# First loads of a recurrent attention and mixture-of-experts kernel, reordered: the first chunk's decay in two transfers, the third chunk's decay ahead of a value tile

## The chip, the cores and the metric

The kernel runs on one core of one Trainium2 chip. The metric is the device time of one execution in microseconds. Of the kernel before, three runs took 281.44, 281.70 and 282.26 us; their median is 281.7 us.

## The reference

There are two stages. The first is a linear attention with a decaying state, for 4 batches, 8 heads, 768 positions and a head size of 48:

```python
for t in range(S):
    cur = einsum('bhd,bhe->bhde', u * k[t], v[t])
    y[t] = einsum('bhd,bhde->bhe', r[t], state + cur)
    state = w[t][..., None] * state + einsum('bhd,bhe->bhde', k[t], v[t])
```

The second takes the 3072 rows of y, 384 wide. A row whose product with `w_skip` is not positive stays as it is. The others go to the one expert of eight with the largest logit of `x @ w_gate`, and get `gate * (relu(x @ w1[e]) @ w2[e])` added, where the gate is that expert's softmax share; the hidden width is 1024.

## The kernel before, in words

**Tiling.** The positions are cut into chunks of 128, six for each batch, 24 in all. `seq` lists them in the order in which they are worked; "chunk 0" below is the first of that list. A chunk has the eight heads as four pairs on 128 partitions. Its arrays w, r, k (`wrk`) lie behind one another in a row: first w (columns 0 to `R_OFF`, 521 words, four groups of `CW` = 130), then r (512 words, up to `K_OFF`), then k (512 words, up to `V_OFF`). Three SBUF buffers `wrk_sb` take chunks in turn; v comes twice, turned (`vt`, two transfers for each chunk) and plain (`v`).

**One chunk's work.** `prep_scan` (L300) runs a backward scan on VectorE (DVE) that makes q, the running product of w. `prep_keys` (L320) makes kq = k*q on GpSimd (POOL) and a reciprocal on DVE that is written into the w tile. `prep_reads` (L327) makes a forward scan rh on DVE and rp = r*rh on POOL. `bonus_keys` (L315) makes rk = r*k on POOL: for chunks 0 and 1 behind rp, for later ones ahead of kq. On TensorE (PE), `scores` (L352) multiplies kq with rp into `psA`, `bonus_sums` (L375) sums rk into `psY`, and `rows_of_keys` (L342) transposes kq, which ScalarE (ACT) copies out as kt. DVE masks the two score tiles (`mask`, L361) and multiplies `psY` with the turned v (`bonus`, L380). `update` (L383) adds to the state from kt and v, `outputs` (L403) adds masked scores times v and state times rp into `psY`, `evict` (L416) copies that out on ACT, and `rows_out` (L421) turns it into rows and router logits by a product with `wgp_sb`, which holds identity columns and router columns.

**Order.** Everything is written by hand: each engine works its instructions in the order of the program. The loop `for s in range(-2, n + 1)` (L681) works on several chunks in one step: it issues loads for chunk s+4 (`load_chunk`) and s+3 (`load_turned`, `load_v`), then update(s), prep_scan(s+2), outputs(s), prep_keys(s+2), prep_reads(s+2), evict(s), scores(s+1), bonus_sums(s+1), rows_of_keys(s+1), the masks and the bonus of s+1, and rows_out(s). So DVE's queue has the scans of chunk s+2 ahead of the masks of chunk s+1. Ahead of the loop, `setup` (L238) issues the loads of chunks 0 to 2 and the memsets, and `fill` (L672) gives PE products of zeros to do. All loads of this stage go through SyncE's (SP) queue, but for u, which is issued from ScalarE.

**Loads at the start, in SP's order.** Chunk 0's w, its r and k in one; chunk 1's w, a table of constants, its r and k; the turned v of chunk 0 in two, its plain v, and chunk 2 in one transfer of 1545 words a row (L178); the router columns in four transfers of 36-byte pieces (L687); turned v and v of chunk 1; chunk 3.

**After the attention** come the router's last products and eight experts, one after the other, with weights split into a high and a low part.

Of the kernel before, what the change touches and what calls it, by code (L numbers as in the profile page):

```python
# [8 lines left out]
F32 = mybir.dt.float32  # L9
# [6 lines left out]
ALU = mybir.AluOpType  # L16
# [5 lines left out]
P = 128  # L22
# [35 lines left out]
def rwkv_moe_kernel(ctx, tc, wrk, wrk0, vN, uP, wgs, wgp, w12, cst, out):  # L58
# [83 lines left out]
    with tc.tile_pool(name="att", bufs=2) as att, \  # L142
# [7 lines left out]
        def half(g, n_=HP):  # L150
            return slice(HP * g, HP * g + n_)

        def shifted(eng, dst, src):

            eng.dma_start(dst[HP:], src[HP:])
            eng.dma_start(dst[KO:HP], src[:D])
            eng.dma_start(dst[:KO], src[D:HP])

        def load_vt(eng, vt, i, o):
            b, c = seq[i]  # L160
            z = wrk[b, c, 0, :, V_OFF + o * 2 * P:V_OFF + (o + 1) * 2 * P]
# [3 lines left out]
        def load_turned(i):  # L165
            for o in range(2):
                load_vt(nc.sync, vt_sb[i % (NBUF + 1)], i, o)

        def load_chunk(i):
            b, c = seq[i]  # L170
            rows = wrk.rearrange("b c g d n -> (b c g d) n")
            at = 2 * D * chunk[i]
            t = wrk_sb[i % NBUF]
            to, at = (t, at - KO) if 0 < chunk[i] < n - 1 else (t[KO:LO], at)
            for cs in (slice(0, R_OFF), slice(R_OFF, V_OFF)) if i < 2 else (slice(0, V_OFF),):
                if i == 1 and cs.start > 0:
                    nc.sync.dma_start(c_sb[:, :C_IOTA], cst[:, :C_IOTA])
                nc.sync.dma_start(to[:, cs], rows[at:at + to.shape[0], cs])  # L178

        def load_v(i):  # L180
            b, c = seq[i]
            v_sb[i] = att.tile([P, H, D], F32, tag="v", name=f"v{i}", bufs=4)
            nc.sync.dma_start(v_sb[i], vN[b, c])
# [11 lines left out]
        identb = keep.tile([P, P], BF16, name="identb")  # L195
        tok = c_sb[:, C_TOK:C_TOK + 2 * B * NC].rearrange("p (c q) -> p c q", q=2)
        rows1_ = c_sb[:, C_HS + 3:C_HS + 4]
        wgp_sb = keep.tile([P, NP, XW], F32, name="wgp_sb")
        wgp_half = wgp_sb.rearrange("p (s g) x -> p g s x", g=2)
        wgs_sb = keep.tile([P, KC, E + 1], F32, name="wgs_sb")  # L200
        ends = keep.tile([P, n, NP], F32, name="ends")
        lows = keep.tile([P, n, NP], F32, name="lows")
# [33 lines left out]
        count_w = scratch(1)  # L236

        def setup():  # L238
            for t in vt_sb[:3]:
                nc.gpsimd.memset(t, 0.0)  # L240
            load_chunk(0)
            load_chunk(1)
            load_turned(0)
            load_v(0)
            load_chunk(2)
            shifted(nc.scalar, u_sb, uP)
            nc.gpsimd.memset(wgp_sb, 0.0)
            nc.gpsimd.memset(vt_sb[3], 0.0)
            nc.gpsimd.memset(onesb, 1.0)
            nc.gpsimd.memset(ohs, 0.0)  # L250
            nc.gpsimd.memset(key, 0.5)
            nc.vector.memset(warm, 0.0)
            nc.vector.memset(pss, 0.0)
            ints = ones_w.bitcast(U32)
            for a in range(NP):
                at = (a + 1) * CW - 1
                nc.vector.memset(ints[:, at // 4:at // 4 + 1], 1 << 8 * (at % 4))
            nc.vector.memset(rowsk, 1.0)
            nc.vector.memset(rowsk[:KO], 0.0)
            nc.vector.memset(rowsk[96:], 0.0)  # L260
            nc.vector.memset(rowsk[96:LO], 1.0)
            nc.vector.tensor_scalar(reads_w.bitcast(U32), ints, rowsk, None, op0=ALU.mult)
            nc.scalar.activation(junk0, warm[:, 0:1], AF.Exp)
            for z in psa:
                nc.scalar.copy(z.rearrange("p a j -> p (a j)"), warm)
            for o in range(2):
                eye = ident[half(o, D), HP * o:HP * o + D]
                for g in range(2):
                    c0 = (o ^ g) * D
                    nc.scalar.copy(wgp_half[half(o, D), g, :, c0:c0 + D],  # L270
                                   eye.rearrange("p (s x) -> p s x", s=1).to_broadcast([D, 2, D]))
            nc.scalar.copy(ubk_sb, u_sb.rearrange("p (a o) -> p a o", o=1).to_broadcast([P, NP, D]))
            for g in range(2):
                nc.tensor.matmul(psy2[:, g].rearrange("p s j -> p (s j)"), warm[:, :P], warm,
                                 start=True, stop=True, skip_group_check=True)
            nc.tensor.matmul(psu.rearrange("p a j -> p (a j)"), warm[:, :P], warm[:, :NP * HP],
                             start=True, stop=True, skip_group_check=True)
# [22 lines left out]
        def prep_scan(i):  # L300
            wk = work[i] = {}
            t = wrk_sb[i % NBUF]
            n_ = NP * CW
            a3 = lambda z: z.rearrange("p (a j) -> p a j", a=NP)
            wk["w"] = t
            wk["r"], wk["k"] = a3(t[:, R_OFF:K_OFF]), a3(t[:, K_OFF:V_OFF])
            q = wk["q"] = att.tile([P, NP, CW], F32, tag="q", name=f"q{i}", bufs=2)
            nc.vector.tensor_tensor_scan(  # L308
                q.rearrange("p a j -> p (a j)")[:, ::-1], t[:, 1:1 + n_][:, ::-1],
                ones_at[:, 1:1 + n_][:, ::-1], 0.0, op0=ALU.mult, op1=ALU.max)  # L310
            rk = wk["rk"] = att.tile([P, NP, P], F32, tag="rk", name=f"rk{i}")
            if i > 1:
                bonus_keys(i)
# [107 lines left out]
        def rows_out(i):  # L421
            psx = work[i]["psx"] = ps1.tile([P, NP, P], F32, tag="psT", name=f"psX{i}", bufs=2)
            xT = work[i]["xT"]
            for a in range(NP):
                nc.tensor.matmul(psx[:, a, :XW], xT[:, a], wgp_sb[:, a], start=True, stop=True)  # L425

        def store(i):
            psx = work.pop(i)["psx"]
# [243 lines left out]
        def fill(k, w=512):  # L672
            psw = ps1.tile([P, 512], F32, tag="psT", name="psw", bufs=2)
            for _ in range(k):
                nc.tensor.matmul(psw[:, :w], warm[:, :P], warm[:, :w], start=True, stop=True)

        with tc.manual_schedule():
# [3 lines left out]
            for s in range(-2, n + 1):  # L681
                on = lambda i: 0 <= i < n
                if s == -2:
                    for o in range(2):
                        for g in range(2):
                            at = 2 * (g ^ o)
                            nc.sync.dma_start(wgp_half[half(o), g, :, 2 * D:],  # L687
                                              wgp[half(g), at:at + 2, 2 * D:])
                if 3 <= s + 4 < n:
                    load_chunk(s + 4)  # L690
                if on(s + 3) and s + 3 >= 1:
                    load_turned(s + 3)
                    load_v(s + 3)
# [413 lines left out]
```

## Time and profile before

| | us |
|---|---|
| median of three runs | 281.7 |
| the profiled execution | 282.66 |
| its span, first to last instruction | 280.8 |
| PE busy in it | 266.0 |
| DVE, ACT, POOL busy | 212.6, 158.1, 146.5 |

The span counts from the first to the last instruction; the execution's own time has 1.86 us more around it. A busy PE counts products of zeros as well, and a product at half the clock counts for as long as it takes. The rows further down have the start of an instruction, counted from the span's start, and its length, both in us; a bracket at the end says how long the engine stood idle ahead of it and which engine's work ended last before it started. That name is inferred.

### The profile page before, as it was taken

The numbers are of one execution on the slowest core, as the hardware profiler recorded it, in microseconds if no ns is written. First come the engines' busy times: TensorE is split into PE (matmuls) and PEld (weight loads), VectorE is DVE, ScalarE is ACT, GpSimd is POOL, SyncE is SP. The second block draws the span as 40 slices with busy tenths as digits, with TensorE's granted clock in tenths as the row PEclk, the third lists the DMA queues.
The fourth block names the chain that finished last, engine by engine and source line by source line (L and its number), as shares of the span: only waits on it lengthen the run. The fifth ranks groups of instructions, "written<-read, shape, count | busy, mean of one in ns | idle before, by whom it ended". The sixth has DMA issues, their size and how long they took to land.

```text
span 280.8 us, 8941 instructions
## 1 busy us (share of the span) xinstructions
PE 266.0 (95%) x3599; PEld 245.0 (87%) x3599; DVE 212.6 (76%) x399; ACT 158.1 (56%) x460; POOL 146.5 (52%) x139
## 2 busy tenths in 40 slices
PE   7879999998999999899999999999999999999992
PEld 2668888897878887787989999999999999999992
DVE  7688999999999999982646787876849578595320
ACT  4436646785688857786427482745818367391300
POOL 6977677798899996894555744011030110301111
PEclk9989999999999999999999999999999999999997
DMA  7999999999977999972058998767563656700001
GB/s 248 231 316 322 314 317 358 358 326 320 277 237 221 303 331 371 254 252 86 30 132 301 350 306 288 243 233 251 180 237 98 247 229 223 250 28 28 9 5 41
DMA packets 26162, 64.23 MB, mean 229 GB/s; under 512 B 4334, under 2 KB 15524, under 8 KB 26112
## 3 DMA queue, kind: packets, MB, share of 16 engines
q1 hardware_dynamic: 23888, 58.27, 63.1%
q0 software_dynamic: 2048, 5.30, 6.1%
q8 instruction: 30, 0.49, 0.7%
q14 instruction: 20, 0.16, 0.2%
q10 hardware_dynamic: 176, 0.00, 0.0%
HBM read 56.52 MB, written 7.67 MB: 229 GB/s over the span
## 4 chain that ended last, share of the span: by engine, by line
PE 59%; issue 5%; ACT 3%; DVE 2%; DMA 1%; POOL 1%; POOLq 0%; DVEq 0%; ACTq 0%
PE psO L915 7%; PE psO L917 6%; PE psO L916 6%; PE psH L890 6%; PE psH L889 6%; PE psH L891 6%; PE psH L135 4%; PE psY L409 3%; PE psX L425 3%; PE psA L358 2%; PE psT L348 2%; PE psY L377 2%; PE psY L413 2%; PE psX L819 2%; DMA xg<-out,idr 1%
## 5 line engine op out<-in xcount | busy, mean ns | idle before, releaser
L826 POOL DMA_INDIRECT out<-fin,ids x16 | 16.6, 1039 | 95.9 <-DVE fin L924 88.9
L896 ACT ACTIVATE hh<-psH 128x240 fp32r<-128x240 f32 (+1 forms) x60 | 22.4, 374 | 53.6 <-PE psH L891 47.6
L890 PE MATMUL psH<-xTl,w1h 128*128 128x240 f32 x168 | 46.3, 275 | 0.0
L889 PE MATMUL psH<-xTh,w1h 128*128 128x240 f32 x168 | 46.1, 275 | 0.0
L891 PE MATMUL psH<-xTh,w1l 128*128 128x240 f32 x168 | 46.1, 274 | 0.0
L915 PE MATMUL psO<-w2h,hh 128*128 128x384 f32 (+1 forms) x120 | 40.9, 341 | 0.0
L917 PE MATMUL psO<-w2h,hl 128*128 128x384 f32 (+1 forms) x120 | 40.3, 335 | 0.0
L916 PE MATMUL psO<-w2l,hh 128*128 128x384 f32 (+1 forms) x120 | 40.2, 335 | 0.0
L364 DVE TENSOR_TENSOR asb<-psA,c_sb 128x512 f32<-128x512 f32 x48 | 30.6, 680 | 5.4 <-PE psA L358 5.2
L901 DVE SCALAR_TENSOR_TENSOR hl<-psH,hh 128x240 fp32r<-128x240 f32 (+1 forms) x60 | 24.3, 405 | 12.7 <-ACT hh L896 8.7
L325 POOL TENSOR_TENSOR kq<-wrk,q 128x512 f32<-128x512 f32 x24 | 28.4, 1185 | 10.0 <-DVE q L308 6.3
L330 DVE TENSOR_TENSOR_SCAN rh<-wrk,rowsk,pss 128x520 f32<-128x520 f32 x24 | 31.1, 1296 | 2.1
L308 DVE TENSOR_TENSOR_SCAN q<-wrk,pss 128x520 f32<-128x520 f32 x24 | 29.5, 1230 | 4.1 <-ACT xT L418 2.2
L334 POOL TENSOR_TENSOR rp<-wrk,rh 128x512 f32<-128x512 f32 x24 | 28.5, 1187 | 6.5 <-DVE rh L330 5.6
L891 PEld LDWEIGHTS psH<-xTh,w1l 128*128 128x128 f32 x168 | 31.8, 189 | 0.0
L889 PEld LDWEIGHTS psH<-xTh,w1h 128*128 128x128 f32 x168 | 31.7, 189 | 0.0
L890 PEld LDWEIGHTS psH<-xTl,w1h 128*128 128x128 f32 x168 | 31.7, 189 | 0.0
L317 POOL TENSOR_TENSOR rk<-wrk 128x512 f32<-128x512 f32 x24 | 30.7, 1278 | 2.0 <-DMA wrk<-wrk 1.6
L409 PE MATMUL psY<-asb,v 128*48 128x128 f32 x384 | 27.1, 277 | 4.4 <-DVE psY L381 4.2
L91 DVE TENSOR_TENSOR w2l<-r,w2h 128x512 fp32r<-128x512 f32 x42 | 27.7, 685 | 1.7 <-ACT w2h L90 1.5
L418 ACT COPY xT<-psY 128x512 f32<-128x512 f32 x24 | 14.1, 588 | 26.0 <-PE psY L413 22.7
L358 PE MATMUL psA<-rp,kq 64*64 64x128 f32 (+1 forms) x768 | 26.6, 256 | 1.4 <-POOL rp L334 1.0
(153 smaller groups left out, 592.7 us busy)
## 6 DMA issues: line engine op xcount, KB each, us to landing
r<-w SPq DMA_DIRECT2D x48, 512.0 KB
wrk<-wrk SPq DMA_DIRECT2D x20, 772.5 KB
vt<-wrk SPq DMA_DIRECT2D x48, 96.0 KB
v<-vN SPq DMA_DIRECT2D x24, 192.0 KB
out<-x SPq DMA_DIRECT2D x24, 192.0 KB
wrk<-wrk SPq DMA_DIRECT2D x2, 579.4 KB
wrk<-wrk SPq DMA_DIRECT2D x2, 512.0 KB
wrk<-wrk SPq DMA_DIRECT2D x2, 260.5 KB
```

The costliest lines, as they stand in the source:

```text
L308: nc.vector.tensor_tensor_scan(q.rearrange("p a j -> p (a j)")[:, ::-1], t[:, 1:1 + n_][:, ::-1], ones_at[:, 1:1 + n_][:, ::-1], 0.0, op0= ...
L317: nc.gpsimd.tensor_tensor(work[i]["rk"].rearrange("p a j -> p (a j)"), t[:, R_OFF:K_OFF], t[:, K_OFF:V_OFF], op=ALU.mult)
L330: nc.vector.tensor_tensor_scan(rh.rearrange("p a j -> p (a j)"), wk["w"][:, 0:NP * CW], reads_at[:, :NP * CW], rowsk, op0=ALU.mult, op1=AL ...
L358: nc.tensor.matmul(psa[g][j:j + HP, a, j:], wk["kq"][rows, a, j:j + HP], wk["rp"][rows, a, j:], start=True, stop=True)
L364: nc.vector.tensor_tensor(s, psa[g], tri.rearrange("p (o j) -> p o j", o=1).to_broadcast([P, NP, P]), op=ALU.mult)
L409: nc.tensor.matmul(y_at(a, g), v[:, 2 * a + g], wk["asb"][g][:, a], start=False, stop=True, skip_group_check=True)
L889: nc.tensor.matmul(ps, w1h[:, o:o + P], xTh[:, kc], start=(kc == 0), stop=False)
L890: nc.tensor.matmul(ps, w1h[:, o:o + P], xTl[:, kc], start=False, stop=False)
L891: nc.tensor.matmul(ps, w1l[:, o:o + P], xTh[:, kc], start=False, stop=(kc == KC - 1))
L915: nc.tensor.matmul(po, h[j, fc][0], w2h[:, o], start=(fc == 0), stop=False)
L916: nc.tensor.matmul(po, h[j, fc][0], w2l[:, o], start=False, stop=False)
L917: nc.tensor.matmul(po, h[j, fc][1], w2h[:, o], start=False, stop=(fc == FC - 1))
```

## The change

The changed kernel cuts chunk 0's `wrk` into four transfers: the first two groups of w, the other two, k, r. The scan that makes q of chunk 0 becomes two scans, one for each half of w. Chunk 2's `wrk` becomes two transfers; its w is issued ahead of the plain v of chunk 0, its r and k behind that v. u is loaded with two transfers in place of three, into a tile that POOL has cleared. The router columns and identity come in three transfers in place of four: for partitions 0 to 63 rows of 840 bytes that hold both, for the others router columns alone, so ScalarE makes two copies of the identity in place of four, and `wgp_sb` changes its layout. The second `fill` of step -1 has three short products in place of two.

```diff
-            for cs in (slice(0, R_OFF), slice(R_OFF, V_OFF)) if i < 2 else (slice(0, V_OFF),):
-                if i == 1 and cs.start > 0:
-                    nc.sync.dma_start(c_sb[:, :C_IOTA], cst[:, :C_IOTA])
-                nc.sync.dma_start(to[:, cs], rows[at:at + to.shape[0], cs])
+        w_half = 1 + NP * CW // 2
+        cuts = {0: ((0, w_half), (w_half, R_OFF), (K_OFF, V_OFF), (R_OFF, K_OFF)),
+                1: ((0, R_OFF), (R_OFF, V_OFF)), 2: ((0, R_OFF), (R_OFF, V_OFF))}
...
+            for c0, c1 in cuts.get(i, ((0, V_OFF),)):
+                yield nc.sync.dma_start(to[:, c0:c1], rows[at:at + to.shape[0], c0:c1])
...
         def setup():
+            nc.gpsimd.memset(u_sb, 0.0)
             for t in vt_sb[:3]:
                 nc.gpsimd.memset(t, 0.0)
-            load_chunk(0)
-            load_chunk(1)
+            drain(load_chunk(0))
+            second, third = load_chunk(1), load_chunk(2)
+            next(second)
+            nc.sync.dma_start(c_sb[:, :C_IOTA], cst[:, :C_IOTA])
+            next(second)
             load_turned(0)
+            next(third)
             load_v(0)
-            load_chunk(2)
-            shifted(nc.scalar, u_sb, uP)
-            nc.gpsimd.memset(wgp_sb, 0.0)
+            next(third)
+            nc.scalar.dma_start(u_sb[HP:LO], uP[HP:LO])
+            nc.scalar.dma_start(u_sb[KO:HP], uP[:D])
+            nc.gpsimd.memset(wgp_sb[HP:], 0.0)
...
-            nc.vector.tensor_tensor_scan(
-                q.rearrange("p a j -> p (a j)")[:, ::-1], t[:, 1:1 + n_][:, ::-1],
-                ones_at[:, 1:1 + n_][:, ::-1], 0.0, op0=ALU.mult, op1=ALU.max)
+            for c0, c1 in ((0, n_),) if i else ((0, n_ // 2), (n_ // 2, n_)):
+                nc.vector.tensor_tensor_scan(
+                    q.rearrange("p a j -> p (a j)")[:, c0:c1][:, ::-1], t[:, 1 + c0:1 + c1][:, ::-1],
+                    ones_at[:, 1 + c0:1 + c1][:, ::-1], 0.0, op0=ALU.mult, op1=ALU.max)
...
-                    for o in range(2):
-                        for g in range(2):
-                            at = 2 * (g ^ o)
-                            nc.sync.dma_start(wgp_half[half(o), g, :, 2 * D:],
-                                              wgp[half(g), at:at + 2, 2 * D:])
+                    z = wgp[half(0), :2]
+                    z = bass.AP(z.tensor, z.offset,
+                                [z.ap[0], [(HP * NP + 2) * XW, 2], [1, 2 * XW]])
+                    nc.sync.dma_start(wgp_sb[half(0)].rearrange("p g s x -> p g (s x)"), z)
+                    for g in range(2):
+                        at = 2 * (g ^ 1)
+                        nc.sync.dma_start(wgp_sb[half(1), g, :, 2 * D:],
+                                          wgp[half(g), at:at + 2, 2 * D:])
...
                     if s == -1:
                         fill(2)
-                        fill(2, 8)
+                        fill(3, 8)
```

## Rows read from the trace of the kernel before

**Rows 1.** By stretch: length; busy PE, PEld, DVE, ACT, POOL; PEclk, DMA share, GB/s.
```profile
12.50:15.00 2.50, 2.50 (x59) 2.31 (x56) 1.80 (x3) 2.37 (x7) 1.83 (x2) 1.00 0.47 90
15.00:18.60 3.60, 1.75 (x33) 1.53 (x34) 3.29 (x5) 0.82 (x5) 2.35 (x3) 0.98 1.05 343
18.60:22.00 3.40, 3.40 (x68) 3.04 (x66) 2.23 (x4) 1.67 (x6) 2.95 (x3) 0.52 1.05 322
22.00:35.00 13.00, 13.00 (x272) 11.47 (x262) 12.12 (x17) 8.38 (x31) 8.75 (x9) 1.00 1.06 321
130.00:275.00 145.00, 144.18 (x1114) 142.34 (x1113) 96.88 (x209) 74.32 (x173) 38.65 (x35) 1.00 0.53 180
```

**Rows 2.** TensorE in order of time, 7 to 30 us.
```profile
7.71 1.09 PE L358 MATMUL psA<-rp,kq 64*64 64x128 f32 x32 [1.03 <-POOL rp L334]
...
10.85 0.61 PE L390 MATMUL psu<-v,kt 128*64 128x48 f32 x15
...
12.32 1.09 PE L358 MATMUL psA<-rp,kq 64*64 64x128 f32 x32
...
15.24 0.67 PE L390 MATMUL psu<-v,kt 128*64 128x48 f32 x16
17.75 1.35 PE L409 MATMUL psY<-asb,v 128*48 128x128 f32 x16 [1.85 <-DVE psY L381]
...
24.13 0.30 PE L409 MATMUL psY<-asb,v 128*48 128x128 f32 x1
...
29.01 0.30 PE L409 MATMUL psY<-asb,v 128*48 128x128 f32 x1
```

**Rows 3.** VectorE in order of time: the scans of q, masks, bonus.
```profile
3.55 1.24 DVE L308 TENSOR_TENSOR_SCAN q<-wrk,pss 128x520 f32<-128x520 f32 x1 [0.51 <-DMA wrk<-wrk]
...
13.06 1.24 DVE L308 TENSOR_TENSOR_SCAN q<-wrk,pss 128x520 f32<-128x520 f32 x1 [2.24 <-ACT xT L418]
...
15.83 1.26 DVE L364 TENSOR_TENSOR asb<-psA,c_sb 128x512 f32<-128x512 f32 x2
17.01 0.69 DVE L381 TENSOR_TENSOR psY<-psY,vt 128x512 f32<-128x512 f32 x1
18.01 1.24 DVE L308 TENSOR_TENSOR_SCAN q<-wrk,pss 128x520 f32<-128x520 f32 x1 [0.31 <-DMA wrk<-wrk]
...
23.70 1.23 DVE L308 TENSOR_TENSOR_SCAN q<-wrk,pss 128x520 f32<-128x520 f32 x1
```

**Rows 4.** GpSimd in order of time: chunk 0's kq, chunk 2's rk.
```profile
5.35 1.17 POOL L325 TENSOR_TENSOR kq<-wrk,q 128x512 f32<-128x512 f32 x1 [2.01 <-DMA wrk<-wrk]
...
13.09 1.27 POOL L317 TENSOR_TENSOR rk<-wrk 128x512 f32<-128x512 f32 x1 [0.70 <-DMA wrk<-wrk]
```

**Rows 5.** SyncE's queue in order of time: loads issued, from chunk 2 on.
```profile
5.42 0.43 SPq L178 DMA_DIRECT2D wrk<-wrk  x1
5.95 3.13 SPq L687 DMA_DIRECT2D wgp_sb<-wgp  x4
9.13 1.06 SPq L163 DMA_DIRECT2D vt<-wrk  x2
10.23 0.43 SPq L183 DMA_DIRECT2D v<-vN  x1
13.02 0.35 SPq L178 DMA_DIRECT2D wrk<-wrk  x1
...
17.95 0.35 SPq L178 DMA_DIRECT2D wrk<-wrk  x1
...
21.56 0.35 SPq L695 DMA_DIRECT2D c_sb<-cst  x1
```

**Rows 6.** ScalarE in order of time: chunk 0's kt.
```profile
10.21 0.59 ACT L350 COPY kt<-psT 128x512 f32<-128x512 f32 x1 [2.15 <-PE psT L348]
```

**Rows 7.** Two stretches of the first loads, columns as in Rows 1.
```profile
3.00:4.50 1.50, 1.50 (x5) 0.58 (x4) 0.99 (x2) 1.49 (x4) 0.34 (x4) 1.00 0.97 361
7.00:8.50 1.50, 0.79 (x30) 0.80 (x32) 1.43 (x3) 1.03 (x6) 1.50 (x2) 1.00 1.17 278
```

More of the change, by code (lines that the diff above doesn't have):

```diff
@@ L151, in half @@
             return slice(HP * g, HP * g + n_)
[L153 to L157, printed above, removed]
         def load_vt(eng, vt, i, o):
@@ L197, in rwkv_moe_kernel @@
         rows1_ = c_sb[:, C_HS + 3:C_HS + 4]
-        wgp_sb = keep.tile([P, NP, XW], F32, name="wgp_sb")
-        wgp_half = wgp_sb.rearrange("p (s g) x -> p g s x", g=2)
+        wgp_sb = keep.tile([P, 2, 2, XW], F32, name="wgp_sb")
         wgs_sb = keep.tile([P, KC, E + 1], F32, name="wgs_sb")
@@ L265, in setup @@
                 nc.scalar.copy(z.rearrange("p a j -> p (a j)"), warm)
-            for o in range(2):
-                eye = ident[half(o, D), HP * o:HP * o + D]
-                for g in range(2):
-                    c0 = (o ^ g) * D
-                    nc.scalar.copy(wgp_half[half(o, D), g, :, c0:c0 + D],
-                                   eye.rearrange("p (s x) -> p s x", s=1).to_broadcast([D, 2, D]))
+            eye = ident[half(1, D), HP:LO]
+            for g in range(2):
+                c0 = (1 - g) * D
+                nc.scalar.copy(wgp_sb[half(1, D), g, :, c0:c0 + D],
+                               eye.rearrange("p (s x) -> p s x", s=1).to_broadcast([D, 2, D]))
             nc.scalar.copy(ubk_sb, u_sb.rearrange("p (a o) -> p a o", o=1).to_broadcast([P, NP, D]))
@@ L424, in rows_out @@
             for a in range(NP):
-                nc.tensor.matmul(psx[:, a, :XW], xT[:, a], wgp_sb[:, a], start=True, stop=True)
+                nc.tensor.matmul(psx[:, a, :XW], xT[:, a], wgp_sb[:, a % 2, a // 2], start=True, stop=True)
         def store(i):
@@ L683, in rwkv_moe_kernel @@
                 if s == -2:
-                    for o in range(2):
-                        for g in range(2):
-                            at = 2 * (g ^ o)
-                            nc.sync.dma_start(wgp_half[half(o), g, :, 2 * D:],
-                                              wgp[half(g), at:at + 2, 2 * D:])
+                    z = wgp[half(0), :2]
+                    z = bass.AP(z.tensor, z.offset,
+                                [z.ap[0], [(HP * NP + 2) * XW, 2], [1, 2 * XW]])
+                    nc.sync.dma_start(wgp_sb[half(0)].rearrange("p g s x -> p g (s x)"), z)
+                    for g in range(2):
+                        at = 2 * (g ^ 1)
+                        nc.sync.dma_start(wgp_sb[half(1), g, :, 2 * D:],
+                                          wgp[half(g), at:at + 2, 2 * D:])
                 if 3 <= s + 4 < n:
-                    load_chunk(s + 4)
+                    drain(load_chunk(s + 4))
                 if on(s + 3) and s + 3 >= 1:
```

## The prediction

> **What bounds the kernel now.** I read the busy times by stretch first. From 130 us on PE is busy for 144.18 of 145 us at the full clock, and from 22 to 35 us for all 13.00 [rows 1]: there PE sets the pace, and a change of the first loads can only move the point at which this begins. Two stretches ahead of it stand out. Between 12.5 and 15.0 us the DMA share is 0.47 and 90 GB/s move, where 321 to 343 move later; and between 15.0 and 18.6 us PE is busy for 1.75 of 3.60 us, behind which its granted clock is 0.52, the lower of its two levels (1.2 of 2.4 GHz), for 3.4 us [rows 1].
>
> PE's order of time names the gap: outputs(1) starts at 17.75 after 1.85 us idle, released by DVE's bonus [rows 2]. On DVE that is one queue: q of chunk 2 at 13.06 after 2.24 us idle, then reciprocal and rh, and only behind them the masks of chunk 1 at 15.83 and its bonus at 17.01, though the scores that they mask were started at 12.32 [rows 2, 3]. The bracket at 13.06 names ACT's xT, but POOL's rk of chunk 2 starts at 13.09 on a DMA, and SP's next load at 13.02 [rows 4, 5]: all three start as chunk 2 lands. So PE's gap is chunk 2's landing.
>
> SP explains the hole in the transfers. The issue at 13.02 (chunk 3) is the eighth after chunk 2's at 5.42 (four, two and one between) and starts when chunk 2 lands; the one at 17.95 is again the eighth after 13.02 and starts as chunk 3 lands, 0.06 us ahead of the scan that waited 0.31 us for it; the one at 21.56 is the eighth after chunk 4's [rows 3, 5]. I read from this that a load waits for the eighth load ahead of it.
>
> The next outputs on PE start at 24.13 and 29.01 [rows 2]. At the full clock a chunk takes 29.01 - 24.13 = 4.88 us; the one of the fall took 24.13 - 17.75 = 6.38. So the fall costs 1.50 us and the gap 1.85: 3.35 us can be had at most, as far as this start goes.
>
> **The change, part by part.**
>
> *Chunk 2's w ahead of chunk 0's v.* The gain: q of chunk 2 no longer waits for 13.06. The price: v of chunk 0 comes later. update(0) starts on PE at 10.85, when kt is out (10.21 + 0.59 = 10.80), so v had landed by 10.85 at the latest [rows 2, 6]; nothing in these rows says by how much sooner. Its new landing: w is 521 words on 128 partitions, 267 KB, at the 361 GB/s of 3.0 to 4.5 us [rows 7] 0.74 us. I take v from 10.4 (my estimate, between 10.1 and 10.85) to 10.4 + 0.74 + 0.2 for the cut of chunk 0 (below) = 11.3. It takes the place of kt as what is late: update(0) moves from 10.85 to 11.35. From there to the end of update(1) PE is continuous, 15.24 + 0.67 - 10.85 = 5.06 us [rows 2], so outputs(1) can start at 16.4. Is DVE in time? w of chunk 2 lands ahead of v, by 11.3; q, reciprocal and rh then take what they took, 15.83 - 13.06 = 2.77, so the masks can start at 14.1 (the scores end at 12.32 + 0.5 + 1.09 = 13.9), and from masks to PE's start it is 17.75 - 15.83 = 1.92 [rows 2, 3]: 16.0. DVE is ready 0.4 us ahead of PE. The gap is gone, and with it, as PE has no pause of that kind left, the fall: the idle 1.03 us ahead of 7.71 was followed by no fall, the 1.85 us was [rows 1, 2]. Outputs(2) could start at 16.4 + 4.88 = 21.3 in place of 24.13.
>
> *Chunk 2's r and k behind v.* About the same bytes lie ahead of their end, so they land near 13.1 to 13.3. POOL then needs rk, kq and rp, three operations of 1.17 to 1.27 us [rows 4]: 17.1 at the latest. PE asks for rp after the first part of outputs(1), not before 16.4 + 1.35 = 17.75 [rows 2]. Cost nothing, with 0.6 us of cover.
>
> *What is late next: chunk 3.* Behind the last part of chunk 2 come three router transfers, two vt and one v, six in all; the eighth load ahead of chunk 3 is then v of chunk 0, not chunk 2's last part. Chunk 3 can be issued at 11.3 in place of 13.02, and the hole is filled: at 321 GB/s [rows 1] 2.5 us move 803 KB, 225 were moved, 578 KB are 1.8 us. Less 0.2 for the cut, chunk 3 lands at 17.95 - 1.6 = 16.35. From the issue of q to PE's outputs it was 17.75 - 13.06 = 4.7 [rows 2, 3], so chunk 3 lets outputs(2) start at 21.05, just ahead of PE's own 21.3. This is the narrowest point of the forecast. Chunk 4 landed by 21.56 and was wanted at 23.70 [rows 3, 5]; moved by 1.6 and 2.8 it keeps 0.9 of its 2.1 us.
>
> *Chunk 0 in four, k ahead of r, two scans.* The first scan started at 3.55 with w; kq at 5.35 with r and k [rows 3, 4]. Half of w can land 0.74/2 = 0.37 us earlier at best, and the second issue stands 0.43 us [rows 5] behind the first, so rp of chunk 0 comes between 0.4 us earlier and 0.3 later; I take 0.2 earlier. It is hidden either way: PE's start at 7.71 moves [rows 2], but update(0) waits for v at 11.3, 0.5 us behind kt; a head late by more than 0.5 us would cost the excess. One more scan costs its fixed share, under 0.1 us of DVE, within the same range. The shorter pieces cost transfer time: w in rows of some 1 KB moves at the 278 GB/s of 7.0 to 8.5 us, where the turned v of 1 KB pieces goes, in place of 361 [rows 7]: 267 KB cost 0.96 for 0.74, the 0.2 above. Bounds: 0, and 0.65 if r and k (524 KB) pay it as well.
>
> The Trainium skill, "DMA: Bandwidth & Descriptors", section "Bandwidth", speaks against such a cut: it tells one to batch transfers to 1 MiB, and its table has 0.95 us for 64 KB and 6.15 for 1 MB. By a line between these, an estimate from that page, two halves of 130 KB take 2.6 us for 2.0, and two of 256 KB 4.0 for 3.4: v 1.2 us later rather than 0.2, and a time of 279.9. The 267 KB in 0.74 us above are no such price, since transfers here follow one another without a pause; the trace before has no pair that differs by the cut alone.
>
> *u in two, router columns in three.* On ACT one issue and two copies less, both ahead of work that waits for others; on SP one issue of 3.13/4 = 0.8 us less [rows 5] while it waits for older loads anyhow. The 840-byte rows carry 98 KB more, 0.3 us at 321 GB/s, against one transfer of small pieces saved; from -0.3 to +0.3 us for what lies behind, and I take 0. One memset and one short product more lie beside waits. Nothing.
>
> *Sum.* 24.13 - 21.3 = 2.8 us at outputs(2). Behind it the order of work stays, each engine's work hangs on the others', and the gain is kept. On the profiled execution 282.66 - 2.8 = 279.9 (span 278.0); that execution is 0.96 us above the median of the runs, and from the median it is **281.7 - 2.8 = 278.9 us**.
>
> **The rivals.**
>
> *A: the stall moves down to chunk 3, and the time is longer.* If a load waits for the last part of the chunk ahead, as chunk 3's issue at 13.02 reads by itself, it stays there, the hole stays, and the cut's 0.2 to 0.65 us and up to 0.3 of the longer router rows come on top: chunk 3 lands at 18.15 to 18.9, outputs(2) could start at 22.85 to 23.6, PE stands idle for 1.6 to 2.3 us as before and the clock falls behind it, 1.50 us more. That is as 24.35 to 25.1 against 24.13, a time of 281.9 to 282.7. It decides from a landing of about 17.9 on. Against it: the count of eight holds at three issues. Chance 0.08.
>
> *B: the transfers give part of it back.* From 22 to 35 us the DMA share is 1.06 [rows 1]. PE moves by 2.8 us, the stream only by 1.6; where a later chunk has under 1.2 us of slack, the gain shrinks to what the stream moved. For it: the share; against it, chunk 4's 2.1 us. Time 281.7 - 1.6 = 280.1. Chance 0.15.
>
> *C: the clock falls elsewhere.* PE's 1.03 us ahead of scores(0) and a new pause ahead of update(0) of up to 0.7 us come closer together. A fall there costs the 1.50 us again: 281.7 - 2.8 + 1.5 = 280.4. Chance 0.10.
>
> *D: it does not do what it says:* the scan waits for all of chunk 2, as for one tile. Then nothing moves but the cut's 0.2: 281.9. Against it: the first scan started 1.8 us ahead of kq, which waited for r and k [rows 3, 4]. Chance 0.03.
>
> **How the numbers follow.** The forecast's mechanism gets 0.58, from 278.3 (v hardly late) to 279.9. Left is 0.06 for an end beyond these cases, half of it no change and half slower. Faster by over 0.3% (0.85 us, what a measurement here can tell from none) is the forecast, B and C: 0.83. Within it 0.12 (D, three quarters of A, half of the rest), slower 0.05. The range reaches over B and C, and 0.4 us below the forecast's low end: 277.9 to 280.9.
>
> **What would show it.** In the changed profile: q of chunk 2 starts at 11 to 11.5 with no wait to 13; update(0) starts near 11.35 and waited for v; outputs(1) near 16.4 with under 0.5 us idle ahead; a granted clock of 1.00 from 15 to 25 us; chunk 3's issue at about 11.3, no stretch under 200 GB/s from 12.5 to 15, its q near 16.4; outputs(2) near 21.3. The forecast is wrong if the 0.5 clock is still there, if chunk 3 is issued at 13 or lands past 17, or if outputs(2) is early and later chunks wait for their loads.

## The result and the profile after

The changed kernel is slower: 283.87 us, the median of 21 runs (281.45 to 289.43), against 281.94 of the kernel before run beside it. The ratio is 1.0062 [1.0037, 1.0087], so 1.7 us more where 2.8 less were forecast. The ratio leaves out three executions of each kernel that took over 1.5% longer than its fastest. The profiled execution took 283.2 us (span 281.4; before 282.66 and 280.8).

By stretch, columns as in [rows 1], to set against [rows 1, 7]; the last line is a longer stretch:

```profile
3.00:4.50 1.50, 1.50 (x5) 0.59 (x4) 1.43 (x4) 1.24 (x4) 0.60 (x4) 1.00 0.96 302
...
12.50:15.00 2.50, 2.48 (x71) 2.31 (x75) 2.36 (x3) 0.90 (x3) 1.66 (x3) 1.00 1.08 241
15.00:18.60 3.60, 3.60 (x70) 3.13 (x66) 2.01 (x4) 2.36 (x9) 3.23 (x3) 1.00 0.95 288
18.60:22.00 3.40, 3.40 (x85) 3.04 (x79) 2.90 (x4) 2.55 (x9) 2.56 (x3) 1.00 1.02 323
22.00:35.00 13.00, 10.42 (x227) 8.95 (x224) 11.49 (x16) 7.04 (x28) 9.56 (x8) 1.00 1.06 303
130.00:275.00 145.00, 144.32 (x1121) 142.50 (x1114) 97.74 (x210) 75.00 (x175) 39.21 (x35) 1.00 0.53 180
...
22.00:72.00 50.00, 46.09 (x1016) 40.30 (x1012) 45.82 (x67) 30.11 (x107) 39.61 (x33) 1.00 1.03 330
```

The same stretch before:

```profile
22.00:72.00 50.00, 48.65 (x1055) 42.58 (x1046) 47.00 (x69) 31.83 (x113) 39.32 (x34) 1.00 1.03 331
```

Both things at which the forecast aimed are gone: from 15.0 to 18.6 us PE is busy throughout, and the clock stays at its upper level. But the first stream is slower (302 GB/s for 361 between 3.0 and 4.5 us), and PE now idles later: 10.42 of 13 us where it had all 13.

TensorE in order of time, as [rows 2]; chunk 0 to chunk 4:

```profile
7.34 1.09 PE L359 MATMUL psA<-rp,kq 64*64 64x128 f32 x32 [0.40 <-POOL rp L335]
...
12.52 0.58 PE L391 MATMUL psu<-v,kt 128*64 128x48 f32 x15 [1.15 <-DMA v<-vN]
...
17.28 0.30 PE L410 MATMUL psY<-asb,v 128*48 128x128 f32 x1
...
23.66 1.08 PE L410 MATMUL psY<-asb,v 128*48 128x128 f32 x16 [1.23 <-DVE psY L382]
...
28.47 0.30 PE L410 MATMUL psY<-asb,v 128*48 128x128 f32 x1
...
32.90 0.42 PE L378 MATMUL psY<-rk,ubk_sb 64*48 64x128 f32 x3 [1.35 <-issue]
...
35.11 0.30 PE L410 MATMUL psY<-asb,v 128*48 128x128 f32 x1
```

Update(0) starts 1.67 us later than in [rows 2] and waited for v. Outputs(1) has no gap ahead of it, yet is only 0.47 us earlier, for it inherits that delay. Ahead of outputs(2) stands a new gap, released by DVE's bonus, as the old one was, one chunk further down. The lead is 0.47 us at outputs(2) and 0.54 at outputs(3). Then PE pauses 1.35 us with "issue" behind it, which is time in which it waited for nothing that the profile names, and outputs(4) at 35.11 is late (33.97 before). The last section says what such a pause waits for.

VectorE's scans of q, as [rows 3], for chunks 0 to 4, and SyncE's loads, as [rows 5]:

```profile
3.07 1.28 DVE L309 TENSOR_TENSOR_SCAN q<-wrk,pss 128x260 f32<-128x260 f32 x2
...
7.80 1.24 DVE L309 TENSOR_TENSOR_SCAN q<-wrk,pss 128x520 f32<-128x520 f32 x1 [1.90 <-DMA wrk<-wrk]
...
12.28 1.23 DVE L309 TENSOR_TENSOR_SCAN q<-wrk,pss 128x520 f32<-128x520 f32 x1
...
18.96 1.24 DVE L309 TENSOR_TENSOR_SCAN q<-wrk,pss 128x520 f32<-128x520 f32 x1 [1.95 <-DMA wrk<-wrk]
...
23.51 1.23 DVE L309 TENSOR_TENSOR_SCAN q<-wrk,pss 128x520 f32<-128x520 f32 x1
```

```profile
5.13 0.43 SPq L174 DMA_DIRECT2D wrk<-wrk  x1
5.60 0.52 SPq L179 DMA_DIRECT2D v<-vN  x1
6.17 0.47 SPq L174 DMA_DIRECT2D wrk<-wrk  x1
...
12.46 0.36 SPq L174 DMA_DIRECT2D wrk<-wrk  x1
```

Chunk 0's scan begins 0.48 us earlier than in [rows 3], as its first half landed early. Chunk 1's w is late for the first time (1.90 us of waiting, until 7.80). Chunk 2's scan no longer waits. Chunk 3 is issued at 12.46, as the v of chunk 0, the eighth load ahead of it, lands (12.38), and so ahead of the 13.02 of [rows 5]; yet its scan starts at 18.96, 0.95 us after the 18.01 of [rows 3].

### The profile page after: what moved, and what is told of

It reads as the page before. It is cut to its first block, busy times and chain, and to the rows that moved or that the text cites. A ratio compares the mean times of both kernels' runs of the same rounds, so it can differ in the third digit from the quotient of the medians.

```text
span 281.4 us, 8944 instructions
## 1 busy us (share of the span) xinstructions
PE 264.8 (94%) x3600; PEld 244.0 (87%) x3600; DVE 212.7 (76%) x400; ACT 157.5 (56%) x458; POOL 147.2 (52%) x140
## 4 chain that ended last, share of the span: by engine, by line
PE 55%; issue 5%; DMA 4%; ACT 3%; DVE 3%; POOL 1%; SPq 0%; POOLq 0%; DVEq 0%; ACTq 0%
PE psO L919 7%; PE psO L921 6%; PE psO L920 6%; PE psH L895 6%; PE psH L893 6%; PE psH L894 6%; PE psH L135 4%; PE psY L410 2%; DMA wrk<-wrk 2%; DMA out<-x 2%; PE psX L426 2%; PE psO L668 2%; PE psX L823 2%; PE psY L378 1%; PE psY L414 1%
## 5 line engine op out<-in xcount | busy, mean ns | idle before, releaser
L830 POOL DMA_INDIRECT out<-fin,ids x16 | 17.2, 1077 | 95.4 <-DVE fin L928 87.9
L309 DVE TENSOR_TENSOR_SCAN q<-wrk,pss 128x520 f32<-128x520 f32 (+1 forms) x25 | 29.6, 1186 | 4.9 <-DMA wrk<-wrk 3.8
L928 DVE SCALAR_TENSOR_TENSOR fin<-psO,gates,xg 128x384 f32<-128x384 f32 (+1 forms) x15 | 9.3, 618 | 23.8 <-PE psO L921 23.8
```

The lines of the kernel that those rows point to most:

```text
L309: nc.vector.tensor_tensor_scan(q.rearrange("p a j -> p (a j)")[:, c0:c1][:, ::-1], t[:, 1 + c0:1 + c1][:, ::-1], ones_at[:, 1 + c0:1 + c1] ...
```

## The experiments

Each ratio is to the kernel before, run beside it. Theory T: the cut of chunk 0 slows the first stream. Theory O, its rival: chunk 2's w ahead of chunk 0's v is what costs. Theory B, for the later runs: what is gained at the start is given back to loads that land when they are due. A profile shows one execution of a kernel, a ratio the median of several.

**The change taken apart.** Four kernels: the change with chunk 0 uncut; before with only the cut; the change with chunk 2 in one piece; before with only chunk 2's w ahead of v.

```diff
 after, chunk 0 uncut (one scan)
-cuts = {0: ((0, w_half), (w_half, R_OFF), (K_OFF, V_OFF), (R_OFF, K_OFF)),
+cuts = {0: ((0, R_OFF), (R_OFF, V_OFF)),
 before, only chunk 0 in four (and two scans)
+four = slice(0, w_half), slice(w_half, R_OFF), slice(K_OFF, V_OFF), slice(R_OFF, K_OFF)
+for cs in four if i == 0 else ...
 after, chunk 2 whole
-        1: ((0, R_OFF), (R_OFF, V_OFF)), 2: ((0, R_OFF), (R_OFF, V_OFF))}
+        1: ((0, R_OFF), (R_OFF, V_OFF))}
...
-            next(third)
             load_v(0)
 before, only chunk 2's w ahead of v
+third = load_chunk(2)
+next(third)
 load_v(0)
+next(third)
```

> The changed kernel with chunk 0's w, and r with k, in one transfer each and one scan, as before; all else changed. Theory T (the pieces): cutting chunk 0's rows into 1 and 2 KB slows the whole stream of the first loads, and this alone moved chunk 0's v and chunk 3 late. Then q of chunk 1 starts near 6.3 (changed kernel 7.80, before 6.25), update(0) near 11.3 (12.52, 10.85), q of chunk 3 near 17 (18.96, 18.01), outputs(2) near 21.5 (23.66, 24.13), and the time is 0.990 to 0.996 of before. Theory O (the order): the w of chunk 2 ahead of chunk 0's v is what costs; then update(0) stays at 12 or later, outputs(2) at 23 or later and the time is 1.000 to 1.008.

> The kernel before with one part of the change alone: chunk 0 in four transfers, k ahead of r, two scans. T: q of chunk 1 at 7.3 to 7.8, update(0) at 11.8 or later, chunk 2 lands near 14.3 in place of 13.0, PE's gap and the fall of the clock stay, outputs(2) near 25.3, time 1.004 to 1.010 of before. O: the start as before within 0.3 us, time 0.998 to 1.002.

> The changed kernel with chunk 2 in one transfer behind chunk 0's v, as before; all else changed. T: the stream is as slow as in the changed kernel and DVE waits for all of chunk 2 (14.3): gap of about 2 us ahead of outputs(1), outputs(2) at 25 or later, time 1.006 to 1.012 of before. O: chunk 0's v lands as before, time 0.998 to 1.002.

> The kernel before with one part of the change alone: chunk 2's w as its own transfer ahead of chunk 0's v, its r and k behind it. T: no small pieces, so v lands by 11.3, q of chunk 2 near 11, no gap ahead of outputs(1), outputs(2) near 21.5, time 0.990 to 0.996 of before. O: v late, update(0) at 12 or later, time 1.002 to 1.008.

Measured: uncut 0.9986 [0.9954, 1.0018]; only the cut 1.0022 [0.9987, 1.0058]; chunk 2 whole 1.0029 [0.9987, 1.0070]; only the order 0.9992 [0.9957, 1.0028]. Without the cut the change costs nothing that can be told, but the order of chunk 2 gains nothing either. All four ratios lie between what T and O asked, so neither theory holds as it was put. The uncut kernel on PE, DVE, SP and by stretch:

```profile
10.88 0.61 PE L391 MATMUL psu<-v,kt 128*64 128x48 f32 x15
...
15.68 0.30 PE L410 MATMUL psY<-asb,v 128*48 128x128 f32 x1
...
22.62 1.08 PE L410 MATMUL psY<-asb,v 128*48 128x128 f32 x16 [1.81 <-DVE psY L382]
```

```profile
10.81 1.23 DVE L309 TENSOR_TENSOR_SCAN q<-wrk,pss 128x520 f32<-128x520 f32 x1
...
17.93 1.24 DVE L309 TENSOR_TENSOR_SCAN q<-wrk,pss 128x520 f32<-128x520 f32 x1 [2.49 <-DMA wrk<-wrk]
```

```profile
10.87 0.37 SPq L174 DMA_DIRECT2D wrk<-wrk  x1
```

```profile
12.50:15.00 2.50, 2.50 (x59) 2.31 (x57) 2.50 (x4) 2.36 (x8) 1.87 (x2) 1.00 1.00 353
...
22.00:72.00 50.00, 47.09 (x1013) 40.60 (x1013) 45.63 (x67) 29.91 (x104) 39.08 (x34) 1.00 1.02 324
```

Chunk 3 is issued 2.15 us earlier than in [rows 5] (10.87 for 13.02), and the hole is filled (353 GB/s for 90); its scan starts 0.08 us earlier (17.93 for 18.01). PE idles 1.81 us for it. The lead of 1.51 us at outputs(2) over the profiled execution of before is 0.07 at the last chunk's outputs, first before, then uncut:

```profile
130.80 1.08 PE L409 MATMUL psY<-asb,v 128*48 128x128 f32 x16 [0.24 <-DVE ohs L630]
```

```profile
130.73 1.08 PE L410 MATMUL psY<-asb,v 128*48 128x128 f32 x16 [0.23 <-DVE ohs L631]
```

Between 22 and 72 us PE was idle for 2.91 us, 2.29 of them behind the start of outputs(2), and before for 1.35.

Update(0) is at 10.88, so without the cut chunk 2's w ahead of v costs it 0.03 us, and the cut adds the other 1.64 of 12.52 - 10.85 = 1.67. But the cut costs that only together with the new order. Update(0) where chunk 0 is cut and chunk 2 stays behind v, first on before, then with chunk 2 whole:

```profile
11.27 0.67 PE L393 MATMUL psu<-v,kt 128*64 128x48 f32 x16
```

```profile
10.86 0.67 PE L390 MATMUL psu<-v,kt 128*64 128x48 f32 x16
```

The landing of chunk 0's v shows why. The trace has sixteen landing records for such a load, and the load is complete with the last of them. Update(0) needs kt as well, which before was out at 10.80 [rows 6], so an earlier v gains nothing:

| kernel | chunk 0 cut | chunk 2's w ahead of v | v complete, us | update(0), us |
|---|---|---|---|---|
| before | no | no | 10.15 | 10.85 |
| before, only the order | no | yes | 10.56 | 10.77 |
| after, chunk 0 uncut | no | yes | 10.38 | 10.88 |
| before, only the cut | yes | no | 10.85 | 11.27 |
| after, chunk 2 whole | yes | no | 10.56 | 10.86 |
| after | yes | yes | 12.38 | 12.52 |
| after, later chunks w first (below) | yes | yes | 11.78 | 11.92 |

Either edit alone makes v 0.2 to 0.7 us later, and update(0) doesn't wait for it (the 11.27 is kt's); both make v 1.6 to 2.2 us later, more than their sum. Why more than the sum is not shown. The ratios agree: with the order the cut takes the kernel from 0.9986 to 1.0062, and the two intervals don't meet; alone on before it has 1.0022, which can't be told from none.

**The cut in its halves.**

```diff
 w in halves only
-cuts = {0: ((0, w_half), (w_half, R_OFF), (K_OFF, V_OFF), (R_OFF, K_OFF)),
+cuts = {0: ((0, w_half), (w_half, R_OFF), (R_OFF, V_OFF)),
 r and k apart only (one scan)
+cuts = {0: ((0, R_OFF), (K_OFF, V_OFF), (R_OFF, K_OFF)),
```

> The changed kernel with chunk 0's w in halves and two scans, its r and k in one transfer. Theory T by size of row: if rows of 1 KB are what slows the stream, q of chunk 1 starts near 7.3 and the time is that of the changed kernel, 1.004 to 1.008; if the cut of r and k counts as much, q of chunk 1 near 6.7 and the time between, 1.000 to 1.004; if w in halves costs nothing, q of chunk 1 at 6.2 to 6.4 and 0.997 to 1.000.

> The changed kernel with chunk 0's w whole (one scan), and its k and r still as two transfers, k ahead. Theory T (each cut of chunk 0 makes the first stream slower, and that is what makes the changed kernel late): the cut of r and k alone costs about half, as the cut of w alone did (1.0030 between 0.9986 uncut and 1.0062 with both cuts): 1.001 to 1.004 of the time before; scores(0) on PE at 7.3 to 8.2 us (7.34 with both cuts, 7.80 uncut), outputs(0) between the 11.29 uncut and the 12.92 of both cuts. Rival W (only the halves of w cost, since they put two short transfers at the very start): 0.997 to 1.000 and outputs(0) at 11.3, as uncut.

Measured: 1.0030 [0.9998, 1.0062] and 1.0047 [1.0018, 1.0077], with update(0) at 11.89 and 11.43 us (uncut 10.88, both cuts 12.52). Each was late at update(0), by 1.01 and 0.55 us, but not by the same wait, so the two don't add up to the 1.64 of both. With w in halves, r and k come later: PE's scores(0) waited, and with them kt, while v was complete at 11.19, ahead of update(0). With r and k apart update(0) waited for v:

```profile
8.60 1.09 PE L359 MATMUL psA<-rp,kq 64*64 64x128 f32 x32 [2.39 <-POOL rp L335]
```

```profile
11.43 0.58 PE L391 MATMUL psu<-v,kt 128*64 128x48 f32 x15 [0.50 <-DMA v<-vN]
```

By the ratios only the cut of r and k is clear of none by itself. How the 0.76% divides between the two stays open.

**Chunk 3.** With chunk 0 uncut: chunk 3 as w | r and k, run twice in separate sets; chunk 3 over 120 rows, so that 15 of the 16 transfer engines carry it (one of its sixteen landing records comes at 11.70 us, 0.58 after the issue, the others from 17.01 on); and, on before and on the uncut kernel, chunks 3 to 23 over the 96 rows that are used of 128.

```diff
 chunk 3 as w | r and k
+3: ((0, R_OFF), (R_OFF, V_OFF))
 120 rows
+if i == 3:
+    to, at = t[4:124], at + 4
 96 rows
-to, at = (t, at - KO) if 0 < chunk[i] < n - 1 else (t[KO:LO], at)
+to, at = (t, at - KO) if i < 3 and 0 < chunk[i] < n - 1 else (t[KO:LO], at)
```

> The changed kernel with chunk 0 uncut, and chunk 3 in two transfers as well, its w ahead of its r and k. Theory W (the stall moved down to chunk 3's landing, as every kernel run so far shows its q at 17.9 or later whatever the issue): q of chunk 3 starts at 15.5 to 16.5 in place of 17.93, the gap of 2 us ahead of outputs(2) goes, outputs(2) at 20.5 to 21 in place of 22.62; if the gain at the start is kept the time is 0.985 to 0.990 of before. Theory G (a gain at the start is given back in the saturated stretch from 25 to 65 us, by stalls of PE for its instructions, which come through the same transfer engines): outputs(2) as early as that, but the kernels are level with before at chunk 10 (62.6), time 0.996 to 1.001.

> The kernel with chunk 0 uncut and chunks 0 to 3 as w | r and k, once more. It had 0.9961 [0.9923, 1.0000]; its profiled run lost the lead of 2.4 us at chunk 2 when chunk 12's scan waited 0.98 us for its transfer and the clock fell behind that. Theory K (the start's gain of about 2 us is kept in most runs, the profiled one was an exception): 0.992 to 0.996. Rival B (the transfers give it back by chunk 13, in every run): 0.997 to 1.000, and a profile with a lead of 1.5 to 2.5 us at outputs(2) that is under 0.8 us at outputs(23).

> The changed kernel with chunk 0 uncut, and chunk 3 loaded over 120 rows in place of 128 (it uses 96 of them), which by the skill's rule on how a transfer is spread go over 15 engines and not 16. Theory L (one of the 16 transfer engines is about 2 us behind the others and sets every landing): if the engine left out is the late one, q of chunk 3 starts near 16 in place of 17.93, outputs(2) near 21. Against it (all engines are equally late, or the late one is another): q of chunk 3 at 17.9 to 18.1, outputs(2) at 22.6.

> The kernel before with chunks 3 to 23 loaded over the 96 rows that are used in place of 128: a quarter less of these bytes, 14% less in all in the attention stage. G: less pressure on the stream, no effect on the start (outputs(2) 24.1 within 0.5), fewer stalls for instructions; time 0.996 to 1.000. If transfers of 96 rows are slower on this chip than of 128, the time is above 1.002.

> The changed kernel with chunk 0 uncut, and chunks 3 to 23 over 96 rows. G: with less pressure the gain of the start is kept: outputs(2) at 22 to 22.5, still 1.5 us or more ahead of before at chunk 10 (61.0 or less), time 0.990 to 0.995. If the gain is lost for another reason than the stream, level with before at chunk 10 and 0.998 to 1.001.

Measured: w first 0.9961 [0.9923, 1.0000] and, again, 1.0017 [0.9987, 1.0048]; 120 rows 1.0061 [1.0019, 1.0102]; 96 rows, seven executions each, 1.0178 [1.0131, 1.0225] on before and 1.0186 [1.0118, 1.0253] on the uncut kernel. Chunk 3's scan started at 17.08 and at 15.47 (no wait) with w first, at 19.01 with 120 rows. A whole chunk 3 of 128 rows, issued anywhere from 10.87 to 13.67 us, had its scan at 17.8 to 19.0 in every kernel here. The second run of w first led by 24.13 - 20.47 = 3.66 us at outputs(2) and was 0.91 behind at the last chunk's (131.71 for 130.80), mostly by three pauses of PE:

```profile
30.87 0.42 PE L379 MATMUL psY<-rk,ubk_sb 64*48 64x128 f32 x3 [1.76 <-issue]
...
44.89 0.67 PE L360 MATMUL psA<-rp,kq 64*64 64x64 f32 x20 [0.67 <-issue]
...
51.62 0.21 PE L360 MATMUL psA<-rp,kq 64*64 64x64 f32 x1 [1.24 <-issue]
```

With "issue" behind them, they make 3.67 us together. The first run lost its lead in another way: chunk 12's scan on DVE waited 0.98 us for its transfer, PE stood idle for 2.29 us ahead of outputs(11), and behind that the clock fell, as the stretch shows:

```profile
62.71 1.24 DVE L310 TENSOR_TENSOR_SCAN q<-wrk,pss 128x520 f32<-128x520 f32 x1 [0.98 <-DMA wrk<-wrk]
```

```profile
68.00:72.00 4.00, 3.83 (x64) 3.48 (x68) 3.50 (x8) 0.58 (x1) 3.37 (x4) 0.57 1.05 342
```

So rival B's outcome held, but not by one and the same wait.

**Fewer bytes, and loads moved.** The kernel with chunk 3's w first, and before, both without the turned-v loads of chunks 4 on; and the former with the experts' first weight loads spread out.

```diff
 no turned v
-load_turned(s + 3)
+if s + 3 < 4:
+    load_turned(s + 3)
 weights spread
-if k0 <= k < k0 + 3:
+if k in ((2, 4, 6) if eq == (0, 1) else range(k0, k0 + 3)):
```

> The changed kernel with chunk 0 uncut and chunk 3's w ahead of its r and k, and without the loads of the turned v from chunk 4 on (those chunks multiply with an older chunk's v, so the bonus part of the output is another): 14% fewer bytes a chunk, the other transfers spread over the engines as before. Theory G (the gain at the start is given back because the loads are saturated from 20 to 65 us: PE waits for its instructions, chunk 12 lands when it is due): no gap over 0.4 us between PE's products from 24 to 65 us other than those of before, at chunk 12 still 1.5 us or more ahead, and a time 0.006 or more below that of the kernel before without the same loads. Against G: level with that kernel within 0.002.

> The kernel before without the loads of the turned v from chunk 4 on (the bonus part of the output is another), as the base for the other. G: the start as before (gap ahead of outputs(1), outputs(2) at 24.1 within 0.4), the later stretch as before within 0.5 us, time 0.996 to 1.000. If the loads bound the kernel throughout, the time is below 0.994.

> The changed kernel with chunk 0 uncut and chunk 3's w ahead, and the three first weight loads (1.5 MB) in every second step in place of three steps in a row. G: chunk 12 lands 1 us or more ahead of its use, the gain at the start is kept to chunk 12 (71.5 or less in place of 73.0), time 0.988 to 0.994 of before. If stalls for instructions take it all the same, 0.995 to 1.000.

Measured: 0.9946 [0.9912, 0.9980], 0.9971 [0.9937, 1.0004] and 1.0008 [0.9968, 1.0048]. The first two differ by 0.25%, between what the two theories asked, and their intervals overlap: inconclusive. Moving the weights did nothing that can be told.

The second of these kernels has the first loads of before, unchanged, and so shows how far one execution of that start is from another. Its chunk 2 was complete at 11.84 us, and 12.94 in the profiled execution of before; outputs(1) and outputs(2) on PE:

```profile
16.66 1.08 PE L409 MATMUL psY<-asb,v 128*48 128x128 f32 x16 [0.91 <-DVE psY L381]
...
22.45 1.08 PE L409 MATMUL psY<-asb,v 128*48 128x128 f32 x16 [0.70 <-DVE psY L381]
```

The gap ahead of outputs(1) is 0.91 us in place of 1.85, the clock stays at 1.00, and outputs(2) starts 1.68 us ahead of 24.13 with nothing reordered, as early as in the uncut kernel (22.62). So the leads given here are leads over one execution with a late start.

**Every chunk with w first.** On the uncut kernel (run twice, in separate sets), on before with nothing else changed, and on the changed kernel with its cut.

```diff
 uncut kernel, every chunk
+cuts = {i: ((0, R_OFF), (R_OFF, V_OFF)) for i in range(n)}
 before, every chunk
-for cs in (slice(0, R_OFF), slice(R_OFF, V_OFF)) if i < 2 else (slice(0, V_OFF),):
+for cs in (slice(0, R_OFF), slice(R_OFF, V_OFF)):
 changed kernel, every chunk from 1 on
-        1: ((0, R_OFF), (R_OFF, V_OFF)), 2: ((0, R_OFF), (R_OFF, V_OFF))}
+        **{i: ((0, R_OFF), (R_OFF, V_OFF)) for i in range(1, n)}}
```

> The same with every chunk as w | r and k, so that a chunk's scan waits for a third of its bytes. Theory B (later chunks take the gain because they land when they are due): with w ahead, a late chunk costs less, the lead of about 2 us is kept: 0.990 to 0.994, and no scan of chunks 4 to 23 waits for a DMA. Rival E (a load waits for the eighth load ahead of it, and with five loads to a chunk in place of four the eighth reaches less far ahead): loads are issued later, more bytes wait, 1.000 to 1.010, with scans or POOL's products waiting for their DMA between 30 and 70 us.

> The fastest kernel so far (chunk 0 uncut, every chunk as w | r and k; 0.9937 [0.9909, 0.9965]) once more, as its neighbour with chunks 0 to 3 so cut had 0.9961 and then 1.0017. If the gain is real: 0.991 to 0.996. If it was this sample: 0.997 to 1.001.

> The kernel before, with nothing changed but that every chunk comes as w | r and k (before: chunks 0 and 1 only); chunk 2 stays behind v of chunk 0. Theory B (whole chunks that land when they are due are what takes a lead away; with w ahead both the start's gain and this count): between 0.994 and 0.999, as w of chunk 2 still lands behind v, 0.002 or more above the 0.9937 of the kernel with w of chunk 2 ahead. Rival L (the gain of 0.6% comes from the later chunks alone, and the start is worth nothing): 0.992 to 0.9945, as that kernel.

> The changed kernel, chunk 0 in four transfers and two scans, with chunks 3 to 23 as w | r and k. Theory T and B (the cut of chunk 0 costs its 0.76% whatever comes behind): 0.999 to 1.003. Rival S (once the later chunks come with w ahead, a late start is caught up as an early one was given back): 0.992 to 0.996, like the kernel with chunk 0 uncut (0.9937).

Measured: uncut 0.9937 [0.9909, 0.9965] and 0.9911 [0.9879, 0.9944], which beats both kernels (279.93 and 279.20 us); before 0.9961 [0.9932, 0.9991]; the changed kernel 0.9950 [0.9923, 0.9978]. The second uncut run, on PE, DVE and by stretch:

```profile
15.59 0.30 PE L409 MATMUL psY<-asb,v 128*48 128x128 f32 x1
...
21.59 1.08 PE L409 MATMUL psY<-asb,v 128*48 128x128 f32 x16 [0.86 <-DVE psY L381]
...
31.28 0.30 PE L409 MATMUL psY<-asb,v 128*48 128x128 f32 x1
```

```profile
16.89 1.24 DVE L308 TENSOR_TENSOR_SCAN q<-wrk,pss 128x520 f32<-128x520 f32 x1 [1.53 <-DMA wrk<-wrk]
```

```profile
22.00:72.00 50.00, 48.63 (x1079) 42.75 (x1075) 47.00 (x71) 31.38 (x113) 42.16 (x36) 1.00 1.02 327
```

Chunk 3's w still makes PE wait 0.86 us, but the lead of 2.54 us at outputs(2) (21.59 for 24.13) is kept: from 22 to 72 us PE idles 1.37 us, as before, no pause there has "issue" behind it, and the span is 277.6, 3.2 us shorter. The profiled execution of the first run, the longest of its twelve (281.98 us), is another picture. Of its lead of 2.96 us at outputs(2) (21.17) 0.42 were left at the last chunk's outputs (130.38), three scans waited for their transfers, against the forecast, and PE idled 3.22 us from 35 to 72 us, where before idled 1.35:

```profile
56.38 1.24 DVE L308 TENSOR_TENSOR_SCAN q<-wrk,pss 128x520 f32<-128x520 f32 x1 [0.71 <-DMA wrk<-wrk]
```

```profile
35.00:72.00 37.00, 33.78 (x723) 29.66 (x721) 34.23 (x53) 22.21 (x79) 30.34 (x27) 1.00 1.03 341
```

So the two ratios are what shows the gain; an execution without pauses is not assured. On before, without chunk 2's w ahead of v:

```profile
10.90 0.61 PE L390 MATMUL psu<-v,kt 128*64 128x48 f32 x15
...
15.69 0.30 PE L409 MATMUL psY<-asb,v 128*48 128x128 f32 x1
...
20.57 0.30 PE L409 MATMUL psY<-asb,v 128*48 128x128 f32 x1
```

```profile
10.81 1.23 DVE L308 TENSOR_TENSOR_SCAN q<-wrk,pss 128x520 f32<-128x520 f32 x1
...
15.35 1.23 DVE L308 TENSOR_TENSOR_SCAN q<-wrk,pss 128x520 f32<-128x520 f32 x1
```

Here neither chunk 2's scan nor chunk 3's waits, and outputs(2) starts at 20.57, 0.7 us ahead of the forecast's 21.3: w ahead of its own r and k was enough, and v needn't give way. Of rival L's claim, that the start is worth nothing, the runs decide little: with the start's order too the ratio is 0.9937 and 0.9911, without it 0.9961, the intervals meet, and this kernel has an early start as well (3.56 us of lead at outputs(2), 2.57 at the last chunk's).

In the changed kernel the later chunks' cut takes 1.0062 to 0.9950, that is 1.1%. The cut of chunk 0 then costs 0.13 to 0.39% (0.9950 against 0.9937 and 0.9911) in place of 0.76% (1.0062 against 0.9986): rival S is nearer than T and B, though the intervals of 0.9950 meet those of both.

## Why the prediction was wrong, point by point

**The gap ahead of outputs(1) and the fall of the clock go: right.** Chunk 2's scan doesn't wait, outputs(1) has no pause, the clock is 1.00 from 15 to 35 us.

**"3.35 us can be had": read off one execution, and taken from the median.** A fall to 0.52 for 3.4 us leaves a mean clock of at most 1 - 0.48 * 3.4 / 280.8 = 0.994; the profiled execution of before has 0.989. Of the 147 executions of before that ran beside the experiments, 123 have 0.995 or more, and so no such fall. The 1.50 us for it were not in the median that the forecast started from. The gap differs too: 0.91 and 0.87 us in the two other profiles with the same first loads (no turned v, and 96 rows on before). How large it is in the median is not known. The prediction had the profiled execution 0.96 us above the median; this may be why.

**The price of the order: too high.** Update(0) was put 0.5 us later, at 11.35; in the uncut kernel it is 10.88 against 10.85. v was complete at 10.15 before, not 10.4, and w ahead of it moved that by 0.23 us in the uncut kernel and 0.41 with the order alone, not by 0.74.

**"Chunk 0 in four": the term that makes the time longer.** It stood at 0.2 us of v's landing, with bounds of 0 and 0.65, and as a price that is added to the order's. Alone the cut made v 0.41 and 0.70 us later, and update(0) didn't wait for it; on top of the order it made it 2.00 later (12.38 for 10.38 in the uncut kernel; 1.40 in the other kernel with both), and update(0) 1.64. The time grew by 0.76%, 2.1 us (1.0062 against 0.9986). The price was formed from GB/s of one row of short pieces [rows 7], for w alone and for a mean rate, where the last part decides. The estimate from the Trainium skill, "DMA: Bandwidth & Descriptors", section "Bandwidth", 1.2 us later, was the nearer one, and in these two executions short too. Its table is of transfers issued from GpSimd, where these are issued from SyncE. I had set it aside because transfers here follow one another without a pause.

**"What is late next: chunk 3": the step that failed even without the cut.** The issue moved as the count of eight says (10.87 in the uncut kernel, forecast 11.3), and the hole was filled. But a landing was worked out as bytes over rate, 17.95 - 1.6, and the landing didn't follow: 17.93. The reader of a load waits for its last part: of the sixteen landing records of chunk 3, fourteen had come by 17.24 us before and by 15.98 in the uncut kernel, the last at 17.89 and 17.81, and the scans started 0.12 us behind that. Filling the hole moved most of the load, not its last part. Which engine is last, and why, stays open: leaving one engine out (120 rows) made it later (18.89).

**"Behind it the gain is kept": wrong.** This was rival B's place. Behind the start of outputs(2) and up to 72 us PE idled 2.29 us in the uncut kernel and 2.68 in the changed one, 1.35 before. With later chunks split the kernels are faster than the same kernels with whole ones: 0.9937 and 0.9911 against 0.9986, and against 0.9961 and 1.0017 with whole chunks from 4 on; 0.9950 against 1.0062; on before 0.9961 against 1. Of the whole ones only the first 0.9961 isn't clear of them. That it is by keeping a lead is less sure: of four profiled executions with every later chunk split one kept all of it, one most (3.56 to 2.57), one grew (0.97 to 1.61), and one lost 2.54 of 2.96 us. Why the split helps is only argued: a scan that waits for 2 KB of a row rather than 6 has reserve against a late part.

**The rivals.** A named the place (a stall moved down to chunk 3) and the sign, but by another road: chunk 3's issue did move, the clock didn't fall, and the cost came with the cut. I gave that 0.08; that its 281.9 to 282.7 came nearer than the forecast is luck. C did not come; D neither. The edits of u and of the router columns are worth nothing that can be told: 0.9992 with the old ones, 0.9986 with the new.

## What to carry to other kernels

Before a stall is priced, ask whether other executions have it: here the mean clocks of the plain runs would have told that most have no fall. Work out a landing from the last part of a load, not from the mean rate: where loads stand in a queue, an earlier issue or a filled hole need not bring the end of a transfer forward. Cut a load where its first third lets work begin (w ahead of r and k, in every chunk), not into more pieces at the head of the stream, where all that follows waits behind them. Don't add up the prices of two edits of one queue without a kernel that has both: each was nearly free here, and together they were not. And look for the gain at the last chunk, not at the first that has it.

## What the runs showed of the hardware that I had not expected

- Loads over 96 rows in place of 128, with a quarter fewer bytes, did not help: chunks 3 to 23 so loaded made the kernel 1.8% slower (1.0178 and 1.0186). Why is not shown.
- The pauses of PE with "issue" behind them end with a fetch of instructions. The twenty profiles have 41 such pauses of 0.3 us or more up to 140 us, and in each PE goes on 1.2 to 1.9 us after the last 16 KB packet of the DMA queue that the profile's page calls "instruction" has ended: at 32.90 in the changed kernel, 1.66 us after one that took 1.53. That the fetch comes late because it shares the transfer engines with the loads is a guess. Without the turned v the engines' share from 22 to 72 us is 0.86 and 0.87 in place of 1.0, and such pauses still make 1.18 and 1.02 us.
- The length of a pause alone did not tell whether the clock falls. Ahead of outputs(1) or outputs(2), 1.85 us [rows 2] and 1.78 us (before, only the cut) were followed by the lower clock; 1.81 (uncut), 2.15 (only the order) and 2.25 us (chunk 2 whole) were not.
- One profiled execution says little of the median: the kernel with only r and k apart showed a span of 279.7, 1.1 us under before, from the shortest of its twelve executions, and its ratio is 1.0047. Two profiles of the same first loads differ by 1.68 us at outputs(2).
